# Pair loads ahead of weight slices: the order of the first DMAs in a fused SSD and FFN kernel

## The chip, the cores and the metric

The kernel runs on one core of one Trainium2 chip. The metric is the device time of one execution in microseconds: the time from the first to the last instruction on that core. The kernel before takes 131.0 us, the median of three runs (130.75 to 131.91). The profile shown here is of one profiled execution; its span is also 131.0 us.

The engines are called by their names in the profile: PE is TensorE (matmul; PEld is its weight load), DVE is VectorE, ACT is ScalarE, POOL is GpSimd, SP is SyncE. SyncE computes nothing here; it issues DMAs. GpSimd both computes and issues DMAs, and each issue takes its place in GpSimd's order of work.

## The reference

Two layers run one after the other. The first is a chunked state-space layer (4 batches, 8 heads, 768 positions, head width 32, state width 16) with a decay `a` for each head and position. The second is a feed-forward layer with squared ReLU on the 3072 tokens of width 256 that the first one gives.

```python
# chunk by chunk of the sequence; state starts at 0
cum = cumsum(log(a))                                   # within the chunk
M = (C @ B^T) * exp(cum_i - cum_j) * causal
y = M @ x + (C @ state) * exp(cum)
state = exp(sum(log a)) * state + sum_j exp(cum_last - cum_j) * B_j x_j
...
x2 = y, transposed to (batch * seq, heads * head_dim)  # 3072 x 256
h = maximum(x2 @ w_in, 0)                              # 256 -> 2048
out = (h * h) @ w_out                                  # 2048 -> 256
```

## The kernel before

The kernel cuts the work into 12 "pairs", each one batch and 256 positions. For pair k it loads C, B and x (float32), and prepares them: `cz` is C times the running product of `a`, `Bb` is B in bf16, `xs` is x divided by that product. Then TensorE transposes B and C (`ph_tr`), makes the states' increments U (`ph_u`), the scores (`ph_mt`), which VectorE masks (`ph_mask`), and the outputs Y (`ph_y`); `ph_s` carries the state on. Y, copied to T in bf16, is the input of one feed-forward block: `mm1` makes two of 16 slices of the hidden layer in each step, ScalarE applies the ReLU, VectorE squares, and `mm2` multiplies with w_out four steps later.

A block takes 8 steps, so there are 96 steps in all, and the work of the next pairs is laid in between by step number. Step f of block 0 uses w_in slices 2f and 2f+1; its `mm2` in step f+4 uses the same slices of w_out.

Loads of a pair go through SyncE's queue, weights through GpSimd's. The weight DMAs convert from float32 to bf16 on the way.

```python

    def ph_load(k, order="CBx", eng=None):
        b, j = PAIRS[k]
        t = loaded.setdefault(k, {})
        for what in order:
            src, w = {"B": (B, N), "C": (C, N), "x": (x, D)}[what]
            dst = nat.tile([128, NH, 2 * w], FP32, tag=f"{what}_nat", name=f"{what}_nat{k}")
            (eng or nc.sync).dma_start(
                out=dst, in_=_dap(src, (b * NH * S + j * 256) * w,
                                  [[2 * w, 128], [S * w, NH], [1, 2 * w]]))
            t[what] = dst

    def load_wi(f0, f1):
        nc.gpsimd.dma_start(
            out=w_in_b[:, :, f0 * 128:f1 * 128],
            in_=_dap(moe_w_in, f0 * 128, [[2048, 128], [128 * 2048, 2], [1, (f1 - f0) * 128]]))

    def load_wo(f0, f1):
        nc.gpsimd.dma_start(
            out=w_out_b[:, f0:f1, :],
            in_=moe_w_out[f0 * 128:f1 * 128, :].rearrange("(f p) d -> p f d", p=128))
    # ... cut ...
    def prep_x(k, eng):
        b, j = PAIRS[k]
        xs = prep.tile([128, 2, 256], BF16, tag="xs", name=f"xs{k}")
        eng.tensor_tensor(
            out=_fap(xs, 0, [[256, 2], [32, 8], [1, 32]]),
            in0=_fap(loaded[k]["x"], 0, [[32, 2], [64, 8], [1, 32]]),
            in1=_fap(Pinv, b * 24 + j, [[96, 2], [3, 8], [0, 32]]), op=ALU.mult)
        live.setdefault(k, {})["xs"] = xs

    def ph_prep(k):
        prep_c(k, nc.gpsimd)
        prep_b(k, nc.gpsimd)
        prep_x(k, nc.gpsimd)
    # ... cut: ph_tr, ph_mt, ph_mask, ph_u, ph_s ...
    # ... end of ph_y(k), which gives T[k]:
        if k < 1:
            for u in range(2):
                o, i = _fap(T[k], u * 64, [[128, 4], [1, 64]]), _fap(Y[u], 0, [[64, 4], [1, 64]])
                if u:
                    nc.vector.tensor_copy(out=o, in_=i)
                else:
                    nc.scalar.copy(out=o, in_=i)
    # ... cut: mm1, square, mm2 ...
```

The program as it is issued, from the first DMA to the end of the prologue, and the plan of the steps:

```python
        nc.sync.dma_start(out=a_nat, in_=_dap(a, 0, [[256, 96], [1, 256]]))
        nc.scalar.dma_start(out=cf, in_=cf_d.ap())
        ph_load(0, "C")
        ph_load(0, "B", nc.scalar)
        ph_load(0, "x")
        nc.gpsimd.dma_start(out=cb, in_=cb_d.ap())
        load_wi(0, 4)
        load_wi(4, 8)
        load_wo(0, 4)
        load_wi(8, 12)
        load_wo(4, 8)
        for k in (1, 2, 3):
            ph_load(k)
        # ... cut: memsets, warm-up matmuls, the decay products P_sb and their reciprocals ...
        nc.scalar.copy(out=P_sb, in_=ptr)
        prep_b(0, nc.scalar)
        nc.scalar.copy(out=Ptot, in_=pps)
        prep_c(0, nc.vector)
        nc.vector.reciprocal(out=_fap(Pinv, 0, [[96, 2], [3, 32]]), in_=_fap(P_sb, 0, [[96, 2], [3, 32]]))
        prep_x(0, nc.gpsimd)
        load_wi(12, 16)
        load_wo(8, 16)
        ph_tr(0)
        warm(5, 128)
        ph_mt(0)
        mtc = big.tile([128, 2, 2, 2, 128], BF16, tag="mtc", name="mtc", bufs=1)
        for i in (1, 0):
            nc.scalar.copy(out=mtc[:, i], in_=live[0]["mt"][1][:, i])
        ph_mask(0, 0)
        ph_u(0)
        warm(14, 128)
        ph_s(0, (0,))
        ph_mask(0, 1)
        ph_mask(0, 3, mtc[:, 1])
        ph_mask(0, 2, mtc[:, 0])
        prep_b(1, nc.scalar)
        prep_c(1, nc.vector)
        prep_x(1, nc.gpsimd)
        ph_y(0)
        ph_s(0, (1,))
        # ... cut ...
        for k in range(1, NPAIR):
            s0 = {1: 0, 2: 7}.get(k, 8 * k - LEAD)
            if k >= 4:
                at(s0 - 15, ph_load, k)
            if k >= 2:
                at(s0 - (5 if k == 2 else 7), ph_prep, k)
            at(s0, ph_tr, k)
            if k <= 2:
                at(s0 + 1, ph_u, k)
            at(s0 + 1 if k <= 2 else s0 - 1, ph_s, k)
            at(s0 + 2, ph_mt, k)
            for q in range(4):
                at(s0 + 2 + (q + 1) // 2, ph_mask, k, q)
            at(s0 + (5 if k == 1 else 6), ph_y, k)
        for s in range(len(steps) + LAG):
            if s < len(steps):
                mm1(*steps[s])
            for fn, args in todo.pop(s, []):
                fn(*args)
            if 1 <= s < len(steps) + 1:
                square(*steps[s - 1])
            if LAG <= s < len(steps):
                mm2(*steps[s - LAG])
        mm2_last(NPAIR - 1, [f for _, f in steps[len(steps) - LAG:]])
```

LEAD is 10 and LAG is 4. `nat` has four buffers for each of B, C and x, so the loads of pairs 0 to 3 wait for nothing, and that of pair 4 waits until pair 0's have been read. `warm(n)` are matmuls on zeros that keep TensorE active. `todo` runs what is planned for a step after that step's `mm1`.

Of the kernel before, what the change touches and what calls it, by code (L numbers as in the profile page):

```python
# [16 lines left out]
def _fap(base: bass.AP, offset_elems: int, free_dims):  # L17

    ap0 = list(base.ap)[0]
    return bass.AP(tensor=base.tensor, offset=base.offset + offset_elems,  # L20
                   ap=[list(ap0)] + [list(d) for d in free_dims])


def _dap(base: bass.AP, offset_elems: int, dims):

    return bass.AP(tensor=base.tensor, offset=base.offset + offset_elems,
                   ap=[list(d) for d in dims])
# [3 lines left out]
def kernel(  # L31
# [78 lines left out]
# [20 lines that stand above are left out]
# [24 lines left out]
# [8 lines that stand above are left out]
# [37 lines left out]
    def ph_mask(k, q, src=None):  # L199
        v = live[k]  # L200
        nc.vector.tensor_tensor(  # L201
            out=v["mts"][:, q], in0=v["mt"][q // 2][:, q % 2] if src is None else src,
            in1=_fap(cb, 128, [[128, 2], [0, 2], [1, 128]]), op=ALU.mult)
# [24 lines left out]
    def ph_s(k, us=(0, 1)):  # L228
        b, j = PAIRS[k]
        v = live[k]  # L230
        U, S_u = v["U"], v["S"]
        for u in us:
            if j == 2 and u == 1:
                break
            ptot = Ptot[:, u, b * 3 + j:b * 3 + j + 1]
            S_n = spool.tile([128, 64], BF16, tag=f"S{b}{u}", name=f"S{k}_{u}")
            if S_u[u] is None:
                nc.vector.tensor_scalar(out=S_n, in0=U[u], scalar1=ptot, scalar2=None, op0=ALU.mult)
            else:
                z = spool.tile([128, 64], FP32, tag="z", name=f"z{k}_{u}")  # L240
                nc.vector.tensor_tensor(out=z, in0=U[u], in1=S_u[u], op=ALU.add)
                nc.vector.tensor_scalar(out=S_n, in0=z, scalar1=ptot, scalar2=None, op0=ALU.mult)
            S_u.append(S_n)
            state[b] = S_n
# [68 lines left out]
    def square(blk, fp):  # L313
        hb = hbs.pop((blk, fp))
        h2 = hpool.tile([128, 2, 256], BF16, tag="h2", name=f"h2{blk}_{fp}")
        nc.vector.tensor_tensor(out=h2, in0=hb, in1=hb, op=ALU.mult)  # L316
        h2s[(blk, fp)] = h2
# [36 lines left out]
    with tc.manual_schedule():  # L354
# [4 lines that stand above are left out]
        ph_load(0, "x")  # L359
        nc.gpsimd.dma_start(out=cb, in_=cb_d.ap())  # L360
        load_wi(0, 4)
        load_wi(4, 8)
        load_wo(0, 4)
        load_wi(8, 12)
        load_wo(4, 8)
        for k in (1, 2, 3):
            ph_load(k)

        nc.vector.memset(dum, 0.0)  # L369
        nc.vector.memset(zer, 0.0)  # L370
        for i in range(3):
            nc.vector.memset(cz[i], 0.0)
        dps = ps_o.tile([128, 256], FP32, tag="ops", name="dps", padded_shape=[128, 512])

        def warm(n, cols=256):
            for _ in range(n):
                nc.tensor.matmul(dps[:, 0:cols], dum[:, 0:128], dum[:, 0:cols],  # L377
                                 start=True, stop=True, skip_group_check=True)

        warm(16)  # L380
        nc.vector.tensor_scalar(out=a_cl, in0=a_nat, scalar1=1e-6, scalar2=1.0, op0=ALU.max, op1=ALU.min)
        for u in range(2):
            nc.vector.tensor_tensor_scan(out=cp_r[:, u * 128:(u + 1) * 128], data0=a_cl[:, u * 128:(u + 1) * 128],
                                         data1=zer, initial=1.0, op0=ALU.mult, op1=ALU.add)
        nc.vector.tensor_tensor(out=pick_p, in0=_fap(pick, 0, [[0, 2], [1, 12]]),
                                in1=_fap(cp_r, 127, [[128, 2], [0, 12]]), op=ALU.mult)
        ptr = ps_h.tile([128, 2, 96], FP32, tag="hps", name="ptr", padded_shape=[128, 2, 256])
        for r in range(2):
            nc.tensor.transpose(ptr[:, r, :], _fap(cp_r, r, [[2, 128]]), eye_f)
        warm(3)  # L390
        pps = ps_h.tile([128, 2, 12], FP32, tag="hps", name="pps", padded_shape=[128, 2, 256])
        nc.tensor.matmul(pps, spread, pick_p, start=True, stop=True)
# [3 lines that stand above are left out]
        prep_c(0, nc.vector)  # L396
        nc.vector.reciprocal(out=_fap(Pinv, 0, [[96, 2], [3, 32]]), in_=_fap(P_sb, 0, [[96, 2], [3, 32]]))
        prep_x(0, nc.gpsimd)
        load_wi(12, 16)
        load_wo(8, 16)  # L400
        ph_tr(0)
        warm(5, 128)
        ph_mt(0)
# [3 lines that stand above are left out]
        ph_mask(0, 0)  # L407
        ph_u(0)
        warm(14, 128)
        ph_s(0, (0,))  # L410
        ph_mask(0, 1)
        ph_mask(0, 3, mtc[:, 1])
        ph_mask(0, 2, mtc[:, 0])
        prep_b(1, nc.scalar)
        prep_c(1, nc.vector)
        prep_x(1, nc.gpsimd)
        ph_y(0)
        ph_s(0, (1,))

        steps = [(b, f) for b in range(NPAIR) for f in range(8)]  # L420
        todo = {}

        def at(s, fn, *args):
            todo.setdefault(max(s, 0), []).append((fn, args))

        def recip_rest():
            nc.vector.reciprocal(out=_fap(Pinv, 1, [[96, 2], [3, 32], [1, 2]]),
                                 in_=_fap(P_sb, 1, [[96, 2], [3, 32], [1, 2]]))

        at(5, recip_rest)  # L430
        for k in range(1, NPAIR):
            s0 = {1: 0, 2: 7}.get(k, 8 * k - LEAD)
            if k >= 4:
                at(s0 - 15, ph_load, k)
            if k >= 2:
                at(s0 - (5 if k == 2 else 7), ph_prep, k)
            at(s0, ph_tr, k)
            if k <= 2:
                at(s0 + 1, ph_u, k)
# [15 lines that stand above are left out]
# [30 lines left out]
```

## Time and profile before

| | before |
|---|---|
| median of three runs | 131.0 us |
| TensorE matmul busy | 114.7 us (88%) |
| VectorE busy | 87.4 us (67%) |
| ScalarE busy | 72.2 us (55%) |
| GpSimd busy | 32.2 us (25%) |
| mean granted TensorE clock | 0.948 of full |
| DMA queue of SyncE (q1) | 38,240 packets, 9.28 MB |
| DMA queue of GpSimd (q0) | 3,232 packets, 2.20 MB (counted in bf16) |
| read from and written to device memory | 10.77 MB and 3.15 MB |

How to read the profile. The page cuts the span into 40 equal slices of 3.28 us and gives for each the busy share of every engine in tenths (9 is 90% or more), the clock that was granted to TensorE, also in tenths, and the mean share of time in which the 16 DMA engines were busy. The chain of waits starts at the last instruction and goes back to whatever released each one, so it names the work that set the end. The timeline lists instructions in order: start, length, engine, source line, operation, tile written from tile read, and in brackets how long the engine had been idle before it and what ended that. A line such as "SPq L116 DMA_DIRECT2D" is the issue of a DMA on SyncE's queue; its length is the time of the issue, [...]and not that of the transfer. The time from issue to landing stands in the view of the DMA issues. A stretch of the busy times gives start and end, length, and then for PE, PEld, DVE, ACT and POOL the busy time with the number of instructions.

The source lines met below: L116 is a pair's load, L122 and L127 the loads of w_in and w_out, L149 and L151 Bb, L137 cz, L157 xs, L219 U, L201 the masks, L276 Y, L293 and L295 T, L306 and L326 the two feed-forward products.

### The profile page before, as it was taken

The numbers are of one execution on the slowest core, as the hardware profiler recorded it, in microseconds if no ns is written. First come the engines' busy times: TensorE is split into PE (matmuls) and PEld (weight loads), VectorE is DVE, ScalarE is ACT, GpSimd is POOL, SyncE is SP. The second block draws the span as 40 slices with busy tenths as digits, with TensorE's granted clock in tenths as the row PEclk, the third lists the DMA queues.
The fourth block names the chain that finished last, engine by engine and source line by source line (L and its number), as shares of the span: only waits on it lengthen the run. The fifth ranks groups of instructions, "written<-read, shape, count | busy, mean of one in ns | idle before, by whom it ended". The sixth has DMA issues, their size and how long they took to land.

```text
span 131.0 us, 4221 instructions
## 1 busy us (share of the span) xinstructions
PE 114.7 (88%) x1778; PEld 92.3 (71%) x1778; DVE 87.4 (67%) x207; ACT 72.2 (55%) x129; POOL 32.2 (25%) x54
## 2 busy tenths in 40 slices
PE   6844073979999999999999999999999999999970
PEld 4533051657887888877878888789778887888850
DVE  3657012897977959779878596696795866945421
ACT  3230031545666766757557667585675675776820
POOL 6753005883005124051070060330330000000000
PEclk9997555699999999999999999999999999999999
DMA  4999997980073290560921724605620020020211
GB/s 94 199 195 200 194 197 142 184 134 0 3 161 85 79 162 11 129 117 0 201 47 54 136 55 120 126 0 121 124 80 8 0 89 1 5 80 0 85 36 44
DMA packets 42788, 12.10 MB, mean 92 GB/s; under 512 B 37808, under 2 KB 41344, under 8 KB 42768
## 3 DMA queue, kind: packets, MB, share of 16 engines
q1 hardware_dynamic: 38240, 9.28, 35.4%
q0 software_dynamic: 3232, 2.20, 11.2%
q10 hardware_dynamic: 1296, 0.35, 1.4%
q8 instruction: 14, 0.23, 0.7%
q14 instruction: 6, 0.05, 0.1%
HBM read 10.77 MB, written 3.15 MB: 106 GB/s over the span
## 4 chain that ended last, share of the span: by engine, by line
PE 73%; DMA 11%; DVE 7%; SPq 3%; POOL 1%; ACT 1%; issue 1%; DVEq 0%
PE ops L326 30%; PE hps L306 29%; DMA x_nat<-in_x_dram 11%; DVE mts L201 4%; PE mt L190 3%; SPq L116 3%; PE Y L276 3%; DVE h L316 3%; PE Y L264 2%; PE tr L178 2%; PE U L219 1%; PE ops L339 1%; PE tr L176 1%; POOL xs L157 1%; ACT hb L310 0%
## 5 line engine op out<-in xcount | busy, mean ns | idle before, releaser
L310 ACT ACTIVATE hb<-hps 128x512 bf16<-128x512 f32 x96 | 57.5, 599 | 37.9 <-PE hps L306 37.6
L306 PE MATMUL hps<-T,w_in_b 128*128 128x256 bf16 x384 | 59.5, 280 | 5.2 <-ACT T L293 5.2
L326 PE MATMUL ops<-w_out_b,h 128*128 128x256 bf16 x368 | 55.5, 273 | 0.0
L316 DVE TENSOR_TENSOR h<-hb 128x512 bf16<-128x512 bf16 x96 | 42.0, 462 | 5.8 <-ACT hb L310 5.8
L306 PEld LDWEIGHTS <-w_in_b 128*128 128x128 bf16 x384 | 38.1, 100 | 10.7 <-issue 5.7
L326 PEld LDWEIGHTS <-h 128*128 128x128 bf16 x368 | 33.8, 98 | 6.1 <-issue 2.0
L201 DVE TENSOR_TENSOR mts<-mt,cb 128x512 bf16<-128x512 f32 x46 | 30.5, 683 | 9.0 <-PE mt L190 8.9
L137 POOL TENSOR_TENSOR cz<-C_nat,P_sb 128x256 bf16<-128x256 f32 x10 | 7.3, 726 | 44.9 <-DMA C_nat<-in_C_dram 38.4
L157 POOL TENSOR_TENSOR xs<-x_nat,Pinv 128x512 bf16<-128x512 f32 x12 | 13.1, 1091 | 17.7 <-DMA x_nat<-in_x_dram 17.4
L180 DVE COPY bct<-tr 128x768 bf16<-128x768 bf16 x12 | 6.7, 558 | 14.0 <-PE tr L178 13.9
L295 ACT CAST T<-Y 128x512 bf16<-128x512 f32 x11 | 6.4, 585 | 2.4 <-PE Y L276 1.6
L276 PE MATMUL Y<-mts,xs 64*32 64x128 bf16 x384 | 6.2, 221 | 1.5 <-DVE mts L201 1.4
L219 PE MATMUL U<-xs,Bb 64*32 64x64 bf16 x160 | 3.5, 199 | 3.6 <-POOL xs L157 3.6
L377 PE MATMUL dps<-dum 128*128 128x256 bf16 (+1 forms) x38 | 5.5, 308 | 1.1 <-DVE dum L369 1.1
L351 ACT COPY osb<-ops 128x512 f32<-128x512 f32 x11 | 6.4, 580 | 0.0
L151 POOL CAST Bb<-B_nat 128x128 bf16<-128x128 f32 x20 | 6.2, 336 | 0.3 <-DMA B_nat<-in_B_dram 0.2
L219 PEld LDWEIGHTS <-Bb 64*32 64x32 bf16 x160 | 2.9, 90 | 4.3 <-issue 4.3
L276 PEld LDWEIGHTS <-xs 64*32 64x32 bf16 x384 | 3.4, 91 | 3.5 <-issue 2.2
L178 PE MATMUL tr<-cb,cz 128*128 128x128 bf16 x48 | 5.6, 227 | 0.0
L190 PE MATMUL mt<-bct 32*64 32x256 bf16 x192 | 5.3, 291 | 0.4 <-DVE bct L180 0.4
L176 PE MATMUL tr<-cb,Bb 128*128 128x128 bf16 x24 | 4.9, 227 | 0.1
L377 PEld LDWEIGHTS <-dum 128*128 128x128 bf16 x38 | 3.7, 119 | 2.0 <-DVE dum L369 1.1
(40 smaller groups left out, 46.5 us busy)
## 6 DMA issues: line engine op xcount, KB each, us to landing
x_nat<-in_x_dram SPq DMA_DIRECT2D x12, 256.0 KB, 4.4
out_dram<-osb SPq DMA_DIRECT2D x11, 256.0 KB, 2.2
C_nat<-in_C_dram SPq DMA_DIRECT2D x12, 128.0 KB, 4.0
B_nat<-in_B_dram SPq DMA_DIRECT2D x11, 128.0 KB, 4.0
w_in_b<-in_moe_w_in_dram POOLq DMA_DIRECT2D x4, 256.0 KB, 8.2
w_out_b<-in_moe_w_out_dram POOLq DMA_DIRECT2D x2, 256.0 KB, 10.3
w_out_b<-in_moe_w_out_dram POOLq DMA_DIRECT2D x1, 512.0 KB, 11.7
B_nat<-in_B_dram ACTq DMA_DIRECT2D x1, 128.0 KB, 4.6
```

Of the source, the lines that this page charges most:

```text
L137: eng.tensor_tensor(out=_fap(czk, 0, [[240, 2], [32, 8], [1, 16]]), in0=_fap(loaded[k]["C"], 0, [[16, 2], [32, 8], [1, 16]]), in1=_fap(P_s ...
L157: eng.tensor_tensor(out=_fap(xs, 0, [[256, 2], [32, 8], [1, 32]]), in0=_fap(loaded[k]["x"], 0, [[32, 2], [64, 8], [1, 32]]), in1=_fap(Pinv ...
L178: nc.tensor.transpose(tr[:, r, 1 + g, :], v["cz"][:, r, 112 * g:112 * g + 128], eye_b)
L190: nc.tensor.matmul(mt[q // 2][64 * u:64 * u + 64, q % 2, r, :, :], bct[32 * q:32 * q + 32, r, 0, u * 64:u * 64 + 64], _fap(bct[32 * q:32 * ...
L201: nc.vector.tensor_tensor(out=v["mts"][:, q], in0=v["mt"][q // 2][:, q % 2] if src is None else src, in1=_fap(cb, 128, [[128, 2], [0, 2], ...
L219: nc.tensor.matmul(U[u][32 * q:32 * q + 32, :], v["Bb"][64 * u:64 * u + 64, r, 32 * q:32 * q + 32], _fap(v["xs"][64 * u:64 * u + 64], r * ...
L276: nc.tensor.matmul(Y[u][32 * q:32 * q + 32, g, :], v["xs"][64 * u:64 * u + 64, r, h * 32:h * 32 + 32], v["mts"][64 * u:64 * u + 64, q, r, ...
L306: nc.tensor.matmul(hps[:, i, :], w_in_b[:, g, f * 128:(f + 1) * 128], T[blk][:, g].rearrange("p r u t -> p (r u t)"), start=(g == 0), stop ...
L310: nc.scalar.activation(out=hb, in_=hps, func=AF.Relu)
L316: nc.vector.tensor_tensor(out=h2, in0=hb, in1=hb, op=ALU.mult)
L326: nc.tensor.matmul(ops[blk][:, r, :], h2[:, i, r * 128:(r + 1) * 128], w_out_b[:, f, :], start=(f == 0 and r == 0), stop=(f == 15), skip_g ...
L377: nc.tensor.matmul(dps[:, 0:cols], dum[:, 0:128], dum[:, 0:cols], start=True, stop=True, skip_group_check=True)
```

## The change

The change only orders. GpSimd issues the constants and the first four slices of w_in as before, but the four weight loads that followed them now stand behind its scaling of pair 0's x, and the last two behind its scaling of pair 1's x. With that the loads of pairs 1, 2 and 3, which SyncE issues, meet fewer weight transfers on the same DMA engines at the start. Besides, VectorE masks the second quarter of pair 0's scores before it makes pair 0's first state, and the preparation of pair 2 is planned one step earlier and that of pair 3 two steps later. No load is dropped or resized, and no arithmetic changes.

```diff
--- before.py
+++ after.py
@@ -359,10 +359,6 @@
         ph_load(0, "x")
         nc.gpsimd.dma_start(out=cb, in_=cb_d.ap())
         load_wi(0, 4)
-        load_wi(4, 8)
-        load_wo(0, 4)
-        load_wi(8, 12)
-        load_wo(4, 8)
         for k in (1, 2, 3):
             ph_load(k)
 
@@ -396,8 +392,10 @@
         prep_c(0, nc.vector)
         nc.vector.reciprocal(out=_fap(Pinv, 0, [[96, 2], [3, 32]]), in_=_fap(P_sb, 0, [[96, 2], [3, 32]]))
         prep_x(0, nc.gpsimd)
-        load_wi(12, 16)
-        load_wo(8, 16)
+        load_wi(4, 8)
+        load_wo(0, 4)
+        load_wi(8, 12)
+        load_wo(4, 8)
         ph_tr(0)
         warm(5, 128)
         ph_mt(0)
@@ -407,13 +405,15 @@
         ph_mask(0, 0)
         ph_u(0)
         warm(14, 128)
+        ph_mask(0, 1)
         ph_s(0, (0,))
-        ph_mask(0, 1)
         ph_mask(0, 3, mtc[:, 1])
         ph_mask(0, 2, mtc[:, 0])
         prep_b(1, nc.scalar)
         prep_c(1, nc.vector)
         prep_x(1, nc.gpsimd)
+        load_wi(12, 16)
+        load_wo(8, 16)
         ph_y(0)
         ph_s(0, (1,))
 
@@ -433,7 +433,7 @@
             if k >= 4:
                 at(s0 - 15, ph_load, k)
             if k >= 2:
-                at(s0 - (5 if k == 2 else 7), ph_prep, k)
+                at(s0 - {2: 6, 3: 5}.get(k, 7), ph_prep, k)
             at(s0, ph_tr, k)
             if k <= 2:
                 at(s0 + 1, ph_u, k)
```

## The prediction

> **What bounds the kernel now.** I read the page's slices first, then the chain of waits over the first 36 us, then the timeline there, then the DMA landings, and last the busy times by stretch. The slices (3.28 us each) show that nearly all slack lies at the start:
>
> ```profile
> PE   6844073979999999999999999999999999999970
> ...
> PEclk9997555699999999999999999999999999999999
> DMA  4999997980073290560921724605620020020211
> ```
>
> From slice 9 TensorE is full to the end. In slices 3 to 8 (10 to 29 us) it is half empty, runs at about half clock, and the DMA engines are at 9 tenths from slice 1 through slice 5. So what can be won lies before about 31 us. The busy times by stretch confirm it (PE, PEld, DVE, ACT, POOL, then the granted clock, DMA share and GB/s):
>
> ```profile
> 12.40:16.90 4.50, 0.00 (x0) 0.08 (x1) 0.25 (x1) 0.77 (x3) 0.00 (x0) 0.50 1.38 195
> 16.90:19.40 2.50, 2.46 (x14) 1.66 (x14) 0.56 (x1) 0.60 (x1) 0.00 (x0) 0.50 1.54 199
> 19.40:21.70 2.30, 0.04 (x1) 0.07 (x1) 0.00 (x0) 0.60 (x1) 1.06 (x1) 0.50 0.73 111
> ...
> 31.30:40.00 8.70, 8.70 (x157) 7.07 (x144) 7.24 (x19) 5.64 (x10) 0.00 (x0) 1.00 0.30 63
> 40.00:131.00 91.00, 86.76 (x1365) 72.05 (x1364) 63.96 (x150) 57.14 (x100) 16.58 (x28) 1.00 0.31 72
> ```
>
> Two holes in TensorE, 4.5 and 2.3 us, with transfers running through both. The chain of waits (start, length, what) names the transfer behind the second:
>
> ```profile
> 5.54 15.00 DMA x_nat<-in_x_dram
> 20.54 0.07 issue
> 20.62 1.07 POOL xs L157
> 21.68 0.04 issue
> 21.72 0.31 PE U L219 x14
> ```
>
> Pair 1's x takes 15.00 us from issue to landing. The timeline shows the first hole and the cause of both:
>
> ```profile
> 7.77 4.35 SPq L116 DMA_DIRECT2D C_nat<-in_C_dram  x1
> ...
> 12.17 4.26 SPq L116 DMA_DIRECT2D B_nat<-in_B_dram  x1
> ...
> 16.12 0.50 ACT L149 CAST Bb<-B_nat 128x128 bf16<-128x128 f32 x2 [6.99 <-DMA B_nat<-in_B_dram]
> 16.52 0.36 ACT L293 CAST T<-Y 128x256 bf16<-128x256 f32 x1
> 16.93 1.01 PE L306 MATMUL hps<-T,w_in_b 128*128 128x256 bf16 x4 [5.17 <-ACT T L293]
> ```
>
> Y of pair 0 is ready at 11.8 (VectorE copies its half to T then), but ScalarE stands first in Bb of pair 1, waiting 6.99 us for B; T's other half comes behind it, and block 0's first matmul at 16.93. SyncE's issues of 4.3 us each are held up by a full DMA.
>
> From the DMA issues, narrowed by time, I get landings (issue plus time to landing). GpSimd's queue: constants 5.6, w_in slices 0-4 at 7.8, w_in 4-8 at 10.3, w_out 0-4 at 12.5, w_in 8-12 at 13.9, w_out 4-8 at 16.3, w_in 12-16 at 17.8, w_out 8-16 at 21.6. SyncE's queue: x of pair 0 at 8.0, C1 10.7, B1 16.1, x1 20.5, C2 22.1, x2 24.1, x3 26.7, pair 4's x 29.4. So a pair load beside weights takes (20.5 - 10.7)/2 = 4.9 us, one after the weights are through (29.4 - 22.1)/8 = 0.91 us, and 256 KB of weights (21.6 - 7.8)/7 = 1.97 us.
>
> **What the Trainium skill says.** "DMA: Bandwidth & Descriptors", section "Queues, rings and completion order": each DMA engine takes the queues it has work for in turn, a packet at a time. The trace agrees: pair loads come in small packets (38,240 packets for 9.28 MB, 243 bytes each), weights in large ones (3,232 for 2.20 MB, 680 bytes), and turn by turn the pair load gets about 0.91/4.9 = 19%. So order of issue, not priority, decides who waits. Same page, "Latency and other measured facts": a GpSimd-issued DMA has its first byte after about 1 us; I use that as an estimate of when weights begin to compete. No row of this trace shows a lone one.
> "TensorE: Matmul & The Clock Gate", section "What's actually happening": the clock is halved or whole by the activity of free-running windows of 3.41 us. The trace agrees: the clock halves at 11.41 and is whole again at 25.06, 13.65 us apart, four windows.
>
> **The change part by part.**
> Order of transfers. GpSimd now issues only the constants and w_in 0-4 at the start; the next weights stand behind its xs of pair 0. That xs needs x of pair 0, whose rivals until 7.8 are the same as before, so it still starts near 8.1 and ends near 9.1 (1.06 us, its row). Four issues of about 0.75 us follow, 9.1 to 12.1; first packets about 10.1. From 8.0 to about 10.1 SyncE's queue is nearly alone: C1 lands 8.9, B1 9.8, x1 10.7 at 0.91 us each, 1.8, 6.3 and 9.8 us earlier.
>
> First hole. Bb of pair 1 runs on ScalarE from 9.8 to 10.3, no longer in the way. On VectorE the second mask goes ahead of S, filling the 0.94 us that it waited for U: masks and C end near 11.0 rather than 11.5. Y ends at 11.2, T at 11.6, first block matmul at 11.6 instead of 16.93: 5.3 us.
>
> Second hole. xs of pair 1 stands behind four weight issues: 12.1 to 13.2. TensorE wants it after two steps and six transposes. In the old trace these took 16.93 to 19.44, 2.5 us at half clock, so wanted at 14.1: no wait. Another 2.3 us, making 7.6, plus up to 2 us if the clock comes back earlier, for the work of 21.7 to 25.1 is at half clock.
>
> What weights give back. Total transfer work is unchanged, so the weights come later. Start from w_in 4-8: issue 9.1 plus 4.4 (the shortest time to landing in GpSimd's queue, the constants') = 13.5, then add the old spacings: w_out 0-4 +2.2 = 15.7; w_in 8-12 +1.4 = 17.1; w_out 4-8 +2.4 = 19.5; w_in 12-16 +1.5 = 21.0; w_out 8-16 +3.8 = 24.8. The second group's issues (13.2 to 14.8) are earlier than their turn, so this order costs no gap.
> Who needs them: w_in 4-8 in step 2, w_in 8-12 in step 4, w_in 12-16 in step 6, w_out 8-16 when step 8 multiplies block 0's fifth pair of slices.
> Steps: mm1 of step 2 at 14.5, full clock by about 15; pair 1's scores end near 16.0. From there the old trace needs 4.5 us to the end of its Y (23.6 to 28.1: four masks with squares between), so 20.5, with the wait for w_in 8-12 (17.1) inside it. Step 6 then begins about 21.0, just as w_in 12-16 lands. Step 8 would begin near 23, and its U needs x2: loads at 4.9 us behind x1, with C2 having a head start, give C2 13.5, B2 18.4, x2 23.3, xs 24.4, U 24.5. Then w_out 8-16 at 24.8. So that fifth pair starts near 25.2 instead of 31.28: 6.1 us won of the 7.6 to 9.6 that the holes offer.
>
> After step 8 the work is the same and TensorE is 96% busy (95.46 of the last 99.7 us), so the 6.1 us carry to the end: 131.0 - 6.1 = 124.9. For the clock I add back 0.4 us: waits in steps 4 to 8 may leave a window too idle; one halved window costs 3.41/2 = 1.7 us, at a chance that I put at one in four. **125.3 us.**
> GpSimd's preps of pairs 2 and 3 a step earlier or two later still fall where it waits for loads; I count nothing.
>
> **The rivals.**
> First: the new wait eats it all. If w_out 8-16, now last in a queue that shares with pairs 2, 3 and 4, lands near 29, when the last pair load lands today, step 8 starts at 29.4 and 129 us result. For: the sum of transfers is the same and its end can't move. Against: the turns favour weights four to one, so pair loads, not weights, are last; today weights finish 7.8 us before the last pair load.
> Second: the weights are not in the way, and the full 7.6 to 9.6 us come: 121.5 to 123.5. For: w_out 8-16 would need to land by 23. Against: 1.5 MB at the measured 1.97 us per 256 KB is 11.8 us after w_in 4-8, so that would have to land at 11.2, two us after its issue.
> Third: a wash or a loss, because GpSimd becomes the bound: its weight issues delay xs of pair 1 and the preps of pair 2. Against: xs of pair 1 has about 0.9 us of slack, and for pair 2 it waits for C and x anyway. Also loads of pair 1 could be slowed by weights starting earlier than 10.1; but even x1 at 13 costs about 1 us only, which step 8's wait hides.
> Fourth: the clock falls again while TensorE waits for slices: 1.7 us for each window, 127 us with one.
>
> **Range and chances.** Landing of w_out 8-16 is the widest term, 23.5 to 27; with the clock it gives 123.2 to 127.4. Over 2% faster means under 128.4, which needs only 2.6 of 6.1 us: 0.92. Within 2%: 0.06 (first rival, with a lost clock window). Slower: 0.02.
>
> **What would show it right or wrong.** Right: B1 and x1 land near 10 and 11, SyncE's issues of 4.3 us come after them; first block matmul near 11.6; xs of pair 1 not in the chain; the chain before 25 us runs through w_out or w_in, or x2; step 8's w_out matmuls near 25. Slice digits of PE from 5 on mostly above 5. Wrong: B1 landing after 12 (loads don't get the engines alone), first matmul after 13, w_out 8-16 after 27, or a half clock that lasts beyond 28. If the stretch after step 8 is longer than the old 99.7 us by over 1 us, the carry to the end is wrong.

## The result, and the profile after

The changed kernel takes 127.84 us (median of four runs, 126.98 to 128.22), the kernel before 131.2 us beside it: a ratio of 0.973, 95% interval 0.966 to 0.980. So it is faster, by more than 2% at the median, but by less than the 5.7 us of the prediction, and 127.84 lies above the range of 123.2 to 127.4.

The time of a run is about 1.8 us longer than the span of its trace: 127.95 against 126.1 for the profiled run of the changed kernel, 132.82 against 131.0 for the one of before. In traces the gain is 131.0 - 126.1 = 4.9 us. So the two figures of 131.0 us for the kernel before, a span and a median time, are not the same thing. The profiled run of before was a slow one (132.82, where the timed runs were 130.75 to 131.91), so the traces make the gain look larger than the times do.

The slices of the changed kernel's page, in tenths:

```profile
PE   6847849999999999999999999999999999999970
...
PEclk9997555599999999999999999999999999999996
DMA  4999999970740733805607408326220020020211
```

TensorE is now full from slice 6 on, not from slice 9. But the clock is still at half in slices 4 to 7, as long as before, and the DMA engines are busy about as long. The same stretches as before (PE, PEld, DVE, ACT, POOL, then clock, DMA share, GB/s):

```profile
12.40:16.90 4.50, 4.10 (x51) 2.27 (x49) 2.41 (x6) 1.79 (x3) 3.56 (x6) 0.50 1.23 181
16.90:19.40 2.50, 0.77 (x4) 0.28 (x3) 2.50 (x6) 0.60 (x1) 1.18 (x1) 0.50 1.59 209
19.40:21.70 2.30, 2.30 (x14) 1.37 (x12) 1.75 (x4) 0.60 (x1) 0.64 (x1) 0.50 1.58 210
```

Of the two old holes, 4.5 and 2.3 us, 0.4 us is left in the first line and nothing in the third. A new one of 1.7 us stands in the middle line, and all three stretches run at half clock. The chain of waits names the hole, and shows the same four products at half and at whole clock (start, length, what):

```profile
9.74 0.75 POOL w_out_b L127
10.48 8.49 DMA w_in_b<-in_moe_w_in_dram
18.98 0.05 issue
19.02 1.03 PE hps L306 x4
...
20.91 0.85 PE hps L306 x4
...
25.18 0.44 PE hps L306 x4
```

Before, the chain went through x of pair 1, 15.00 us from issue to landing. Now it goes through w_in 8-12, issued at 10.48 and landed 8.49 us later. The timeline has the places that the prediction gave times for:

```profile
9.59 0.50 ACT L149 CAST Bb<-B_nat 128x128 bf16<-128x128 f32 x2 [0.84 <-DMA B_nat<-in_B_dram]
...
11.57 1.01 PE L306 MATMUL hps<-T,w_in_b 128*128 128x256 bf16 x4 [0.69 <-DVE z L241]
...
19.02 1.03 PE L306 MATMUL hps<-T,w_in_b 128*128 128x256 bf16 x4 [1.73 <-DMA w_in_b<-in_moe_w_in_dram]
...
26.94 0.61 PE L326 MATMUL ops<-w_out_b,h 128*128 128x256 bf16 x4
```

B of pair 1 is there at 9.6 (before: 16.1), and block 0 starts at 11.57 (before: 16.93). The last line is the w_out product of step 8, at 26.94 (before: 31.28). So of the 5.4 us won at the first product, 1.0 us is lost again by step 8. From step 8 to the end the trace needs 99.1 us (before: 99.7).

The landings, read from the DMA issues as in the prediction: C1 8.7, B1 9.6, x1 10.8, C2 11.7, B2 12.5, x2 17.1; w_in 4-8 at 14.7, w_out 0-4 at 17.6, w_in 8-12 at 19.0, w_out 4-8 at 20.5, w_in 12-16 at 21.9, w_out 8-16 at 25.3.

### The profile page after: what moved, and what is told of

Same layout as the page of the kernel before. It is cut to its first block, busy times and chain, and to the rows that moved or that the text cites. A ratio compares the mean times of both kernels' runs of the same rounds, so it can differ in the third digit from the quotient of the medians.

```text
span 126.1 us, 4221 instructions
## 1 busy us (share of the span) xinstructions
PE 115.9 (92%) x1778; PEld 92.7 (74%) x1778; DVE 85.9 (68%) x207; ACT 72.4 (57%) x129; POOL 32.0 (25%) x54
## 4 chain that ended last, share of the span: by engine, by line
PE 81%; DMA 12%; POOL 2%; ACT 1%; DVE 1%; SPq 1%; issue 0%; DVEq 0%; POOLq 0%
PE ops L326 34%; PE hps L306 33%; DMA w_in_b<-in_moe_w_in_dram 7%; DMA x_nat<-in_x_dram 5%; PE Y L276 3%; PE mt L190 3%; PE Y L264 3%; PE tr L178 2%; PE ops L339 1%; PE U L219 1%; PE tr L176 1%; POOL xs L157 1%; POOL w_out_b L127 1%; POOL w_in_b L122 1%; ACT hb L310 0%
## 5 line engine op out<-in xcount | busy, mean ns | idle before, releaser
L306 PE MATMUL hps<-T,w_in_b 128*128 128x256 bf16 x384 | 60.7, 283 | 2.8 <-DMA w_in_b<-in_moe_w_in_dram 1.7
L326 PE MATMUL ops<-w_out_b,h 128*128 128x256 bf16 x368 | 56.7, 278 | 0.0
L316 DVE TENSOR_TENSOR h<-hb 128x512 bf16<-128x512 bf16 x96 | 40.5, 446 | 7.0 <-ACT hb L310 7.0
L326 PEld LDWEIGHTS <-h 128*128 128x128 bf16 x368 | 34.3, 99 | 6.7 <-issue 2.2
L137 POOL TENSOR_TENSOR cz<-C_nat,P_sb 128x256 bf16<-128x256 f32 x10 | 6.7, 669 | 42.3 <-DMA C_nat<-in_C_dram 30.3
L157 POOL TENSOR_TENSOR xs<-x_nat,Pinv 128x512 bf16<-128x512 f32 x12 | 13.4, 1116 | 11.6 <-DMA x_nat<-in_x_dram 11.1
L180 DVE COPY bct<-tr 128x768 bf16<-128x768 bf16 x12 | 6.7, 558 | 12.5 <-PE tr L178 12.2
L276 PE MATMUL Y<-mts,xs 64*32 64x128 bf16 x384 | 5.3, 226 | 0.0
L242 DVE TENSOR_SCALAR S<-z,Ptot 128x64 bf16<-128x64 f32 x16 | 4.4, 273 | 0.6
L241 DVE TENSOR_TENSOR z<-U,S 128x64 f32<-128x64 f32 x16 | 3.6, 223 | 1.7 <-PE U L219 1.2
## 6 DMA issues: line engine op xcount, KB each, us to landing
w_out_b<-in_moe_w_out_dram POOLq DMA_DIRECT2D x1, 512.0 KB, 11.6
```

The lines of the kernel that those rows point to most:

```text
L137: eng.tensor_tensor(out=_fap(czk, 0, [[240, 2], [32, 8], [1, 16]]), in0=_fap(loaded[k]["C"], 0, [[16, 2], [32, 8], [1, 16]]), in1=_fap(P_s ...
L157: eng.tensor_tensor(out=_fap(xs, 0, [[256, 2], [32, 8], [1, 32]]), in0=_fap(loaded[k]["x"], 0, [[32, 2], [64, 8], [1, 32]]), in1=_fap(Pinv ...
L180: nc.vector.tensor_copy(out=bct, in_=tr)
L276: nc.tensor.matmul(Y[u][32 * q:32 * q + 32, g, :], v["xs"][64 * u:64 * u + 64, r, h * 32:h * 32 + 32], v["mts"][64 * u:64 * u + 64, q, r, ...
L306: nc.tensor.matmul(hps[:, i, :], w_in_b[:, g, f * 128:(f + 1) * 128], T[blk][:, g].rearrange("p r u t -> p (r u t)"), start=(g == 0), stop ...
L326: nc.tensor.matmul(ops[blk][:, r, :], h2[:, i, r * 128:(r + 1) * 128], w_out_b[:, f, :], start=(f == 0 and r == 0), stop=(f == 15), skip_g ...
```

## The experiments

Two theories stood against each other. L: the weights now start too late, and their landing sets step 8 and with it the end. C: TensorE's half clock up to 24.9 us sets it. "Step 8" below is the start of that step's first w_out product. Ratios are to the kernel before, run beside each experiment, with 95% intervals. Each diff is against the changed kernel unless it says otherwise.

**e1: the kernel before, once more.** No edit.

> The kernel before, unchanged, profiled once more. Theory A (the old trace was of a run with an unusually long half clock, so that its start was worse than usual): the span of the trace is 129 to 129.6 us instead of 131.0, and step 8's first w_out product starts 1 to 1.7 us before 31.28. Theory B (the trace was typical and the gain was truly 4.9 us): span 130.5 to 131.3 and step 8 at 31.0 to 31.5. Ratio of times 1.00 in both.

Ratio 0.998 (0.995 to 1.001), as it must be for the same program. The trace has a span of 130.5 us and step 8 at 30.96. That is theory B, at its lower edge. But this trace, too, is of a run above its median (132.24 for 131.59), and no trace of a faster run of this kernel is kept: with the 99.5 us that both traces need behind step 8, a run of 131.6 us would have step 8 near 30.3 (an estimate, 131.6 less 1.8 and 99.5). The clock differs: half for 17.1 us here, for 13.65 us in the first trace. What that costs can be read from the runs of this kernel beside all experiments, e1's included: 11 of 70 had a granted clock of 0.99 or more over the whole run, and their mean is 131.9 us, as is that of the other 59 (0.92 to 0.95). In the kernel before, half clock falls where TensorE waits anyway.

**e2: w_in 8-12 ahead of w_out 0-4.**

```diff
-        load_wo(0, 4)
         load_wi(8, 12)
+        load_wo(0, 4)
```

> The changed kernel with w_in 8-12 issued ahead of w_out 0-4. Theory W (step 4's wait of 1.7 us for w_in 8-12 sets the end): that slice lands near 16.5 to 17 instead of 19.0, the wait goes, step 8 starts 1 to 1.7 us earlier, time 126.2 to 126.8. Theory C (TensorE at half clock from 11.3 to 24.9 us, and w_out 8-16 landing at 25.3, set the end): the wait goes but step 8 comes less than 0.8 us earlier, time 127.1 to 127.9.

Ratio 0.968 (0.962 to 0.973), against 0.973 and (in e5) 0.969 for the changed kernel: no difference that these runs can tell, and inside theory C's forecast. The wait for w_in 8-12 in step 4 is gone and the clock is whole again at 21.7 instead of 24.9, but step 8 comes at 26.25 and now waits for the slices behind (timeline of e2, then its chain of waits):

```profile
26.25 0.60 PE L326 MATMUL ops<-w_out_b,h 128*128 128x256 bf16 x4 [0.49 <-DMA w_out_b<-in_moe_w_out_dram]
```

```profile
13.78 12.43 DMA w_out_b<-in_moe_w_out_dram
26.21 0.04 issue
```

Here w_out 8-16 landed at 26.2. So taking step 4's wait away is not enough: with it gone and the whole clock earlier, the step ran into the next landing.

**e3: warm-up products where TensorE waits.** Zeros only; the outputs are the same.

```diff
         ph_mask(0, 0)
+        warm(10)
         ph_u(0)
         ...
         ph_y(0)
+        warm(5)
```

> The changed kernel with 15 more warm-up products on zeros, where TensorE waits: ten before U of pair 0 and five behind Y of pair 0. Theory C (half clock costs the end): the clock stays whole beyond 11.3 us, steps 0 to 2 run at whole clock until they wait for weights, and if it stays so step 8 starts near 25.4 (w_out 8-16 at 25.3), time 126.3 to 127. Theory W (waits for weights set the end whatever the clock): whole clock at the start, longer waits in steps 2 and 4, step 8 not more than 0.5 us earlier, time 127.4 to 128.

Ratio 0.970 (0.964 to 0.976): no gain. The clock did stay whole in steps 0 to 3, as the page of e3 shows:

```profile
PEclk9999985599999999999999999999999999999999
```

It bought longer waits: 1.79 us for w_in 4-8 in step 2 and 2.64 us for w_in 8-12 in step 4. In the second the clock fell (18.1 to 24.9 at half), and step 8 came at 27.31. Theory C's 25.4 is missed, and theory W's forecast holds: keeping the clock up ahead of the waits for data only lengthened the waits here.

**e4: the order of the DMAs alone.** The mask, the state and the preparations of pairs 2 and 3 as before the change.

```diff
-        ph_mask(0, 1)
         ph_s(0, (0,))
+        ph_mask(0, 1)
         ...
-                at(s0 - {2: 6, 3: 5}.get(k, 7), ph_prep, k)
+                at(s0 - (5 if k == 2 else 7), ph_prep, k)
```

> Only the new order of the DMAs; the mask, the state and the preparations of pairs 2 and 3 stand as before. All theories: nearly the whole gain is the order's, 127.6 to 128.4; the first block product comes 0.2 to 0.5 us later than 11.57, and step 4 still waits for w_in 8-12 until 19.0, which hides that. A rival, that the mask and the preparations carry a third of the gain or more: 129 or above.

Ratio 0.967 (0.961 to 0.973): the whole gain is the order's. Block 0 started at 12.72, 1.15 us later than in the changed kernel (0.2 to 0.5 were expected), and step 8 still came at 26.14, with w_out 8-16 landed at 26.0. A lost microsecond at the start costs nothing while the weights decide.

**e5: the changed kernel again**, for comparison on the same chip as e6 to e8.

> The changed kernel, unchanged, beside the next three on one chip. Ratio to the kernel before 0.966 to 0.975; step 8's first w_out product between 26.1 and 27.3 us; w_in 8-12 awaited until near 19.

Ratio 0.969 (0.964 to 0.974). w_out 8-16 landed at 25.8, step 8 at 26.78, w_in 8-12 awaited until 19.3.

**e6: w_in 4-8 at the start again.**

```diff
         load_wi(0, 4)
+        load_wi(4, 8)
         ...
         prep_x(0, nc.gpsimd)
-        load_wi(4, 8)
         load_wo(0, 4)
```

> The changed kernel with w_in 4-8 issued at the start again, behind w_in 0-4; only the three others wait for xs of pair 0. Theory L (the weights' late start and their 1.9 to 2 us per 256 KB set the end): w_in 4-8 lands near 9.7, the last slices, w_out 8-16, near 23.3 to 24 instead of 25.3; B1 and x1 land 1.5 to 2 us later; step 8 at 24.8 to 25.8; time 1 to 1.8 us under the changed kernel. Rival C (half clock alone sets step 8): weights land earlier, step 8 within 0.4 us of the changed kernel's. Rival S (the start cannot bear it): first block product at 13 or later and step 8 not earlier.

Ratio 0.957 (0.952 to 0.961), 125.93 us against 128.02 for the changed kernel beside it. The direction is theory L's, though its numbers were missed by a little (23.3 to 24, 24.8 to 25.8 and 1 to 1.8 us): the last slices landed at 24.15 and step 8 came at 24.19, though block 0 started at 12.89 and not at 12.04 as in e5. The timeline of e6:

```profile
10.90 0.50 ACT L149 CAST Bb<-B_nat 128x128 bf16<-128x128 f32 x2 [2.06 <-DMA B_nat<-in_B_dram]
...
12.89 1.01 PE L306 MATMUL hps<-T,w_in_b 128*128 128x256 bf16 x4 [0.67 <-DVE z L241]
...
24.19 0.60 PE L326 MATMUL ops<-w_out_b,h 128*128 128x256 bf16 x4 [0.44 <-DVE S L238]
```

The bracket of the last line names S of pair 2, which was done at 24.16; but the product reads w_out and h and not S, so what it waited for is w_out 8-16. B1 lands 1.3 us later than in the changed kernel, and step 8 still comes 2.6 us sooner than in e5. Half clock, 6.83 us for 13.65 in e5, may have a part in that. This version beats both kernels.

**e7: pairs 3 and 4 through GpSimd's queue, behind all weights.**

```diff
-        for k in (1, 2, 3):
+        for k in (1, 2):
             ph_load(k)
         ...
-            if k >= 4:
+            if k in (3, 4):
+                at(2 * k - 3, ph_load, k, "CBx", nc.gpsimd)
+            elif k >= 5:
                 at(s0 - 15, ph_load, k)
```

> The changed kernel, but pairs 3 and 4 are loaded through GpSimd's own queue behind all weights, so that after x2 nothing of SyncE's shares the DMA engines with them. Theory L2 (sharing with pairs 3 and 4 costs the weights a quarter of their rate): w_out 8-16 lands near 22.5 to 23.5 instead of 25.3. Theory R (the weights run at near 1.8 us per 256 KB alone too, being large packets): it lands at 24 to 25. Time equal to the changed kernel's within 0.5 us under R, up to 1 us less under L2.

w_out 8-16 landed at 24.6, within theory R and short of L2: 10.5 us after its issue, where it took 11.8 in e5. But theory R's reason does not hold. From the landing of w_out 0-4 (17.75; in e5 17.95) to that of w_out 8-16, 256 KB of weights took (24.58 - 17.75)/5 = 1.37 us without pair loads beside them, not 1.8, and (25.82 - 17.95)/5 = 1.57 us with them in e5. So sharing costs the weights about an eighth of their rate, not a quarter. Ratio 0.962 (0.957 to 0.968); its interval overlaps e5's.

**e8: e2, e6 and e7 together.** The three edits above.

> All three together: w_in 4-8 at the start, w_in 8-12 ahead of w_out 0-4, pairs 3 and 4 behind the weights. Theory L: no wait for weights but small ones, step 8 at 23.7 to 25, time 124.8 to 126.2 or 2 us under the changed kernel. Theory C: not more than 0.6 us under it.

Ratio 0.971 (0.965 to 0.976): the time, 127.83 us for 128.02 in e5, is that of theory C, but not for its reason. Step 8 came at 23.87, as L has it, and the gain was lost right behind it. The stretch of e8 from 27 to 31 us, and GpSimd's timeline:

```profile
27.00:31.00 4.00, 2.42 (x58) 1.86 (x56) 2.58 (x5) 2.76 (x5) 4.00 (x7) 1.00 0.90 199
```

```profile
22.18 1.07 POOL L157 TENSOR_TENSOR xs<-x_nat,Pinv 128x512 bf16<-128x512 f32 x1 [4.87 <-DMA x_nat<-in_x_dram]
23.19 0.95 POOL L116 DMA_DIRECT2D C_nat<-in_C_dram  x1
```

TensorE is idle for 1.6 of these 4 us. With the weights earlier, x2 came at 22.1 instead of 16.6 in e7; GpSimd waits for it before it issues pair 3's load at 23.2, whose x lands near 29.7. A load behind a computing engine's wait is as late as that wait.

**e9 and e12: four extra loads of 256 KB of w_in** into tiles that nothing reads, e9 in steps 20 and 34, e12 in step 80.

```diff
+        at(20, probe, 0)
+        at(34, probe, 1, 2, 3)      # e12: at(80, probe, 0, 1, 2, 3)
```

> The changed kernel with four extra loads of 256 KB of w_in into tiles that nothing reads, from GpSimd's queue while the DMA engines are idle: one alone in step 20 (near 40 us) and three together in step 34 (near 56 us). Theory Q (a lone weight load has a short lag, 3.5 to 4.4 us, and the 5.7 us at 9 us came of sharing with the pair loads): the lone one lands 3.5 to 4.4 us after its issue. Theory D (the lag is GpSimd's own, before a byte moves): 5 us or more. The three together give the rate without rivals: 1.2 to 1.4 us apart if sharing cost a third of it, 1.7 to 2 us if not.

> The same four extra loads of 256 KB of w_in, now one behind the other at about 91 us, when the last pair load has landed and only a 256 KB store comes beside them. Theory Q (a weight load alone has a short lag, 3.5 to 4.4 us; the 5.7 us at 9 us came of sharing): the first lands 3.5 to 4.4 us after its issue, the others 1.1 to 1.5 us apart. Theory D (the lag is the queue's own): the first lands 5 us or more after its issue, the others 1.6 to 2 us apart, as beside the pair loads.

e9 missed its quiet places: GpSimd runs ahead of TensorE, so the loads were issued at 31.3 and 47.4, and pair loads began within 2 us of each. They landed 6.0 us after issue (the one alone) and 5.2 us (the first of three), the three 1.9 us apart on average. In e12 the loads were issued from 91.80 on, with one store beside them. The DMA issue of the first, and the stretches from 92 us:

```profile
probe<-in_moe_w_in_dram POOLq DMA_DIRECT2D x1, 256.0 KB, 4.8
```

```profile
92.50:93.00 0.50, 0.50 (x47) 0.31 (x36) 0.50 (x3) 0.50 (x2) 0.50 (x2) 1.00 0.00 0
93.00:93.50 0.50, 0.50 (x40) 0.44 (x16) 0.50 (x3) 0.29 (x2) 0.50 (x2) 1.00 0.45 25
...
94.50:95.00 0.50, 0.50 (x7) 0.44 (x6) 0.00 (x0) 0.38 (x1) 0.22 (x1) 1.00 1.08 145
95.00:95.50 0.50, 0.50 (x10) 0.49 (x8) 0.00 (x1) 0.34 (x1) 0.00 (x0) 1.00 1.20 219
...
99.00:99.50 0.50, 0.50 (x7) 0.44 (x6) 0.50 (x2) 0.22 (x2) 0.00 (x0) 1.00 1.28 211
```

The last two numbers of a line are the DMA share and GB/s. GpSimd's queue moves its first packet at 93.26, 1.5 us after the issue, and little for 1.2 us more; 200 GB/s, the store's share in it, are reached 3.2 us after the issue. The first load lands after 4.8 us, just under theory D's 5 and above Q's 4.4. The others land at 99.7, 101.0 and 102.3. That is (102.3 - 96.6)/3 = 1.9 us a load, as theory D has it, but the gaps are unlike: 3.1, 1.3 and 1.2 us. In the first the store still ran, which landed at 97.4; in the other two only the weight loads do, at up to 211 GB/s (last line), and there theory Q's rate holds, as in e7. Why the queue was still slow from 97 to 98 us (113 to 135 GB/s), when the store's data had moved, is open.

**e10: the four weight loads behind xs of pair 1 too.**

```diff
         prep_x(0, nc.gpsimd)
-        load_wi(4, 8)
-        load_wo(0, 4)
-        load_wi(8, 12)
-        load_wo(4, 8)
         ...
         prep_x(1, nc.gpsimd)
+        load_wi(4, 8)
+        load_wo(0, 4)
+        load_wi(8, 12)
+        load_wo(4, 8)
         load_wi(12, 16)
```

> The changed kernel with the four weight loads behind xs of pair 1 as well, so that all but w_in 0-4 are issued 3 to 4 us later (near 13 instead of 9). Theory L (the weights' late start sets the end): w_out 8-16 lands 2.5 to 4 us later, near 28 to 29.5, step 8 at 28.5 to 30, time 2 to 3.5 us over the changed kernel, ratio to the kernel before 0.985 to 1.0. Theory C (half clock sets it): less than 1 us over the changed kernel.

Ratio 0.988 (0.982 to 0.994), against 0.969 in e5: 0.019 x 131.6 = 2.5 us above the changed kernel; w_out 8-16 landed at 28.7 and step 8 came at 28.70. Theory L's numbers hold. Weight loads that start 3 us later end 3 us later, and the end follows. It follows by an earlier slice, though: the chain of e10 goes through w_in 8-12, and from there to step 8 TensorE has no hole.

```profile
13.48 7.82 DMA w_in_b<-in_moe_w_in_dram
21.29 0.05 issue
```

**e11: e6's order, with the other parts as before the change (e4's edit).**

> The DMA order with w_in 4-8 at the start, and the mask, the state and the preparations of pairs 2 and 3 as before the change. If those parts do nothing: the same as with them, ratio 0.952 to 0.961, step 8 within 0.5 us of 24.2. If the preparation of pair 2 a step earlier matters now that x2 comes late: 0.5 to 1 us slower.

Ratio 0.956 (0.951 to 0.960), step 8 at 24.98 with the last slices landed at 24.93. The mask, the state and the two preparations do nothing that can be measured, in this order of loads either.

All traces side by side (us; half clock is the sum of half-clock time from 8 to 29 us):

| kernel | w_out 8-16 landed | step 8 | half clock | ratio |
|---|---|---|---|---|
| before / e1 | 21.6 / 21.6 | 31.28 / 30.96 | 13.65 / 17.07 | 1 / 0.998 |
| changed / e5 | 25.3 / 25.8 | 26.94 / 26.78 | 13.65 / 13.65 | 0.973 / 0.969 |
| changed, with later extra loads: e9 / e12 | 27.05 / 26.3 | 27.09 / 26.93 | 13.65 / 10.24 | one run each |
| e2 w_in 8-12 first | 26.2 | 26.25 | 10.24 | 0.968 |
| e3 warm | 26.0 | 27.31 | 6.83 | 0.970 |
| e4 order alone | 26.0 | 26.14 | 10.24 | 0.967 |
| e6 w_in 4-8 at start | 24.15 | 24.19 | 6.83 | 0.957 |
| e7 pairs 3, 4 behind | 24.6 | 25.79 | 13.65 | 0.962 |
| e8 three together | 23.83 | 23.87 | 3.41 | 0.971 |
| e10 behind x1 | 28.7 | 28.70 | 17.07 | 0.988 |
| e11 e6, plain | 24.93 | 24.98 | 6.83 | 0.956 |

Apart from the kernel before, step 8 comes within 0.15 us of the landing in seven traces of twelve. In the other five, where half clock ended less than 2.3 us before the landing, it comes 0.6 to 1.6 us behind. That TensorE stood idle for w_out 8-16 is seen in four of the traces only: 0.49 us in e2, 0.44 in e6, 0.26 in e9 and 0.23 in e11. In the others it was at work right up to step 8. In the changed kernel it works without a break from the end of its wait for w_in 8-12, at 19.02, to step 8 at 26.94, and at half clock until 24.9. The chain above has 0.85 us for a step's four products at half clock and 0.44 us at whole clock, so at whole clock those 5.9 us would be near 3 (an estimate), and step 8 would have met the landing at 25.3.

So when the weights land decides: e6 and e10 move the weights, and step 8 and the end move with them. That half clock adds up to 1.6 us on top is read from the traces; no run takes half clock away and leaves the landings as they were.

## Why the prediction was right and wrong

**Right: the mechanism.** Weights held the pair loads up, and the new order takes B1 and x1 out of their way: predicted 9.8 and 10.7, landed 9.6 and 10.8. The first block product: predicted 11.6, came at 11.57 (11.6 to 12.9 over all kernels with the new order; the same program has it at 12.04 in e5, so the last tenths are luck). xs of pair 1 is in no wait. The new chain runs through the weights. In the traces 4.9 of the 5.7 us are there. Not shown is that SyncE's long issues "are held up by a full DMA": in the changed kernel C2's issue took 0.58 us at 7.60, with the DMA engines at 9 tenths there too.

**Wrong: the start of the weights.** The step that failed is "Start from w_in 4-8: issue 9.1 plus 4.4 ... = 13.5", with "first packets about 10.1" and "w_out 8-16 +3.8 = 24.8" behind it. The loads were issued at 8.98, as said, but w_in 4-8 needed 5.7 us (5.8 to 6.3 in e2 to e5), not 4.4, and landed at 14.7. The first packet of GpSimd's queue came at 11.04 and not at 10.1: 2.1 us after the issue, where the prediction had taken 1. The 4.4 was the constants' time, 96 KB; w_in 0-4, a load of 256 KB on the same queue, took 5.8 us in the very trace of before that the prediction read. Over the traces of the new orders the first of the loads held back took 5.0 to 6.3 us. The late start also shows in the pair loads: x1, C2 and B2 still came 0.7 to 0.9 us apart up to 12.5, 3.5 us after the first weight issue. The later landings were late too. w_in 8-12 came at 19.0 instead of 17.1, and the new chain goes through it. w_out 8-16 came at 25.3, and at 25.8 to 27.05 in the other traces whose first loads are in the changed kernel's order or e2's (e2 to e5, e9, e12): 0.5 to 2.3 us late.

**Wrong: "full clock by about 15".** The clock was halved at 11.24 and whole at 24.90. I took it that steps 0 to 2 at work would bring it back. In the free-running windows of 3.41 us that the prediction took from the Trainium skill ("TensorE: Matmul & The Clock Gate", section "What's actually happening"), TensorE was busy 2.74, 2.58 and 2.46 us in the first three, and 3.41 in the fourth: only after that one was the clock whole. The new wait for w_in 8-12, 1.7 us, is one reason why windows stayed short. Step 8 came 1.6 us behind the landing of w_out 8-16, where the prediction has 0.4 and adds 0.4 for the clock; that half clock makes the difference is the reading of the traces above, not an experiment's.

**Wrong: the zero point.** "131.0 - 6.1 = 124.9" takes a gain out of a trace whose span of 131.0 us is a time of 132.82, and applies it to the median time, which is 131.0 by chance. The trace's gain was 4.9 us; the times give 131.2 - 127.84 = 3.4, and 0.969 in e5 makes it 131.57 x 0.031 = 4.1. So 0.8 to 1.5 us of the miss is not the kernel's doing. Held against the span that it was worked out from, the prediction is 125.3 us, and the span of the changed kernel is 126.1.

The sum, in the traces: step 8 was predicted at 25.2 and came at 26.94, 1.7 us late, 0.5 of it by the landing (25.3 for 24.8) and 1.2 between landing and step (1.6 for 0.4). The 0.4 us added for the clock covers a part, and behind step 8 a further 0.5 us was won that was not predicted and is not explained. That leaves 0.8 us. The rest of the 2.5 us between 125.3 and 127.84 is the zero point: 1.5 us between the trace's gain and that of the times, and 0.2 us between the medians of before, 131.0 and 131.2.

**The rivals.** The first (weights take all) was the right kind of wait with too large a size. The second (full 7.6 to 9.6 us) needed w_out 8-16 by 23, and it landed at 25.3: from w_in 4-8 on, 256 KB took (25.3 - 14.7)/6 = 1.8 us, near the 1.97 of before. That "the turns favour weights four to one" agrees in kind with e7: without pair loads the weights come 1.37 us apart, with them 1.57 (e5). The third (GpSimd as bound) fell for the changed kernel, but e8 built it: there GpSimd's wait for x2 held the next loads. The fourth (clock) came in another form: in the changed kernel the old half clock did not fall a second time but lasted four windows again, at a cost that the traces put at up to 1.6 us.

x2 was predicted at 23.3 and landed at 17.1: C2 and B2 had already come, at 11.7 and 12.5, in the weights' slow start.

## What to carry to other kernels

When transfers are reordered, write down for each one the step that first needs it and the earliest time that its queue can land it: total work on the DMA engines does not shrink, and what is put last becomes the next wait. Of the orders tried here the best was not all pair loads first but one weight load kept ahead (e6), which delayed block 0 by 0.9 us and brought the end 2 us forward, both against e5. And compare trace with trace and time with time; a span and a median that happen to agree are not the same number.

## What the runs showed of the hardware

- A GpSimd-issued 256 KB load that converts to bf16 moved nothing for 1.5 us, reached 200 GB/s (a store included) after 3.2 us and landed after 4.8 us, with only that store beside it (e12). In the changed kernel, beside pair loads, its first packet came 2.1 us after the issue. What fills this time, the writing of descriptors or the engines, was not taken apart.
- Such loads, queued one behind the other, landed 1.57 us apart beside pair loads (e5), 1.37 without them (e7), and 1.3 and 1.2 with nothing else on the DMA engines (the last two of e12).
- Half clock came in whole windows: 3.41, 6.83, 10.24, 13.65 and 17.07 us, one to five times 3.41. In all fourteen traces it ended after windows with TensorE busy 3.00 us and more of 3.41, but once after one of 2.75 us (e12), and it went on after windows of up to 3.07 us (e5). So TensorE's busy time alone does not tell when it ends.
- The same program got four and five such windows (before, e1), at spans of 131.0 and 130.5 us, and its runs without half clock took as long as those with it. So half clock while TensorE waits for data anyway costs little.
